# First tiles of a four-layer attention and MLP kernel: VectorE order, load order, one tile's transpose and the weight loads

## The chip, the cores and the metric

The kernel runs on one core of a Trainium2 chip. The metric is device time of one execution in microseconds (us). Before the change the median of 3 runs is 758.88 us (758.61 to 761.05).

The engines are TensorE (PE, matrix products; PEld is its weight load), VectorE (DVE), ScalarE (ACT), GpSimd (POOL) and SyncE (SP), which issues the DMAs here. Each engine takes its instructions in order, so an instruction that waits holds up all that stand behind it on its engine.

## The reference

`x` has 2048 rows of 576 values in bf16. Four layers follow one another, attention (A), MLP (B), A, B, all with the same weights, each on a layer norm of its input and with a residual sum:

```
def _A_ref(x, wqkv, wo):
    q, k, v = ...            # x @ wqkv, 32 heads of 18
    phi = lambda t: jnp.where(t > 0, t + 1, jnp.exp(t)) + 1e-6
    pq, pk = phi(q), phi(k)
    kv = jnp.einsum("bhsd,bhse->bhde", pk, v)
    z = jnp.einsum("bhsd->bhd", pk)
    num = jnp.einsum("bhqd,bhde->bhqe", pq, kv)
    den = jnp.einsum("bhqd,bhd->bhq", pq, z)[..., None] + 1e-6
    o = num / den
    return o... @ wo

def _B_ref(x, w1, b1, w2, b2):
    h = _gelu(jnp.einsum("bsd,df->bsf", _layernorm(x), w1) + b1)
    return jnp.einsum("bsf,fd->bsd", h, w2) + b2

x = x + _A_ref(_layernorm(x), A_wqkv, A_wo)
x = x + _B_ref(_layernorm(x), B_w1, B_b1, B_w2, B_b2)
...                          # the same two once more
```

## The kernel before

The rows are cut into 16 tiles of 128 (NT). Products over the 576 features need the normalised rows turned, features on the partitions: `yT` holds them in 5 blocks of 128 (KD). Layer 1 (li = 0) reads its rows from the input; each tile goes through a small pipeline, `LNPipe`, whose `tick` moves every tile in it one step on: statistics (DVE: two bn_stats and one bn_aggr, L391, L392, L398; or ACT: two passes that sum, L371 and L381), the reciprocal deviation (ACT with Ln and Exp for tiles 0 to 2, L422 and L424; else POOL with a power, L427), the normalisation (DVE for tiles 0 to 3, L440; POOL for the others, L436), and the turning. A tile below `XB` is turned by five PE transposes into PSUM (L494), which ACT copies to `yT` (L500); the others by one DMA transpose on SP (L483). `feed0` (L1162) puts a tile of layer 1 in and chooses its path.

Per tile layer 1 then makes the keys in two halves (`k_half`, five products each, L657), the feature map of the keys (an exponential on ACT, L544, and one maximum and minimum on DVE, L546), and, one tile later, the sums of rows by keys (`rows_by_keys`, L699: four chunks of 128 features and a tail, `k2_tail`). Between them stands one of the 20 query products (`q_proj`, five products, L625), with an exponential (L558) and an identity pass (L559) on ACT, both read from PSUM, and a minimum and a maximum on DVE (L564, L566). The query, key and transpose results share the four PSUM buffers of pool `ps_h`; the tail of the sums holds one of them to the end of the keys. A product whose turn comes needs a buffer that its last reader has left.

For the first tiles the order is written out by hand: instructions are entered under names (`s2a`, `s2b`, `g2`, `u2` for the statistics of tile 2, `n2` for its normalisation, `cd0` and `ca0` for the copies of tile 0's transposes, `e10` and `ma10` for the exponential and the maximum of tile 1's first key half), and `in_order` (L181) makes each follow the one before it. PE has its own written order (`pe`). `chained` (L160) does the same for the DMA issues of the beginning.

SP issues the loads: row tiles and the key, query and value weights first; then the DMA transposes in turn with `late_pieces` (L264), one of which `pre_a1_layer0` (L1177) takes off per tile from tile 4 on: nine pieces of w1 of 512 KB, the output weight `piece_wo`, two w1 tails, the first three pieces of w2, b1; b2 goes at the last tile. `last_pieces`, the last three of w2, went one by one at the last four tiles of layer 1's output stage (L1016). An issue also waits until the DMA eight issues before it has landed, since the DMAs take turns on eight semaphores.

After the keys come the sums of the second half, the denominators, the products of keys and values with the output weight (`kv_wo_half`, L769), the output products (L968) and the residual sums. The MLP then works on chunks of 512 rows: 9 groups of first products (`m1_group`, L1082) and second products over 36 blocks of the hidden values (L1144).

## Time and profile before

| | |
|---|---|
| median of 3 runs | 758.88 us |
| the profiled execution | 759.16 us |
| its span | 757.2 us |
| PE busy in the span | 750.6 us |
| DVE, ACT, POOL busy | 261.3, 323.3, 114.9 us |
| granted TensorE clock | 1.00 in the stages of layer 1 |
| DMA moved | 75.20 MB |

The span is that of the traced instructions; the profiled execution's own time is 1.92 us longer. In a row of the timeline stand the start, the duration of a run of equal instructions, engine, line, operation, what is written and read, and the count; in brackets the idle time of the engine just before and what ended it. A run of PE's reaches past the start of the next one, because products overlap. SPq rows are issues of DMAs, not the transfers. In the rows by stage each engine has its busy time and count, and at the end stand the granted clock, the mean busy share of the DMA engines and GB/s.

### The profile page before, as it was taken

Reading aid. Unit: us, or ns where it says so; the run is one execution under the profiler, and the core shown is the slowest. Engines: PE = TensorE matmul, PEld = TensorE weight load, DVE = VectorE, ACT = ScalarE, POOL = GpSimd, SP = SyncE. Lnnn points to the kernel's source line nnn. Section 1 sums busy time; section 2 is a strip of 40 time slices with the busy share of each in tenths; the row PEclk is TensorE's granted clock in tenths of the full one; section 3 lists DMA queues with packets and bytes.
Section 4 is the critical chain, followed back from the end, with each engine's and each line's share of the span. In section 5 each row is a group of like instructions: output and inputs, shape, how many; then the busy total and the mean of one; then the engine's idle time right before and its main releaser. Section 6 shows DMA issues by size and latency. Waiting matters only on the chain.

```text
span 757.2 us, 15677 instructions
## 1 busy us (share of the span) xinstructions
PE 750.6 (99%) x6555; PEld 484.7 (64%) x6555; DVE 261.3 (35%) x641; ACT 323.3 (43%) x722; POOL 114.9 (15%) x219
## 2 busy tenths in 40 slices
PE   8999999999999999999999999999999999999998
PEld 5677754774476457646777777457646754774476
DVE  7766824136034403401366567600230132000000
ACT  5767656105601640373057666660174036205600
POOL 4830313003010201200110004300020020001000
PEclk9999999999999999999999999999999999999999
DMA  8796692226313611411404147430240033011000
GB/s 241 172 246 159 200 350 65 71 65 182 82 40 94 166 51 48 121 54 32 127 24 118 32 137 256 173 83 16 87 106 17 16 126 83 9 32 56 1 9 24
DMA packets 83984, 75.20 MB, mean 99 GB/s; under 512 B 39882, under 2 KB 68554, under 8 KB 83914
## 3 DMA queue, kind: packets, MB, share of 16 engines
q1 hardware_dynamic: 83914, 74.21, 34.5%
q8 instruction: 51, 0.84, 0.5%
q14 instruction: 19, 0.16, 0.1%
HBM read 48.10 MB, written 24.77 MB: 96 GB/s over the span
## 4 chain that ended last, share of the span: by engine, by line
PE 95%; DMA 1%; ACT 1%; DVE 1%; POOL 1%; SPq 0%; issue 0%; POOLq 0%; DVEq 0%
PE m_ps L1144 36%; PE h_ps L1082 21%; PE hp_ps L1082 16%; PE q_ps L625 5%; PE k_ps L657 5%; PE k_ps L699 4%; PE wo_ps L968 3%; PE m_half L1144 1%; DMA xo<-x_d 1%; DMA x<-in_A_x_dram 1%; PE k_tail L699 0%; PE kv_ps L751 0%; ACT turned L846 0%; PE rden_ps L842 0%; PE den_ps L801 0%
## 5 line engine op out<-in xcount | busy, mean ns | idle before, releaser
L1144 PE MATMUL m_ps<-w_sb,hT 128*128 128x288 bf16 x2232 | 274.8, 286 | 0.0
L1144 PEld LDWEIGHTS <-hT 128*128 128x128 bf16 x2304 | 224.2, 98 | 60.4 <-issue 3.4
L1082 PEld LDWEIGHTS <-w_sb 64*128 64x128 bf16 x2304 | 124.5, 94 | 136.4 <-issue 1.9
L1082 PE MATMUL hp_ps<-yT,w_sb 64*128 64x512 bf16 x1152 | 178.0, 376 | 0.0
L1082 PE MATMUL h_ps<-yT,w_sb 64*128 64x512 bf16 x1152 | 148.0, 376 | 0.0
L1087 ACT COPY relay_sb<-relay_sb 128x1 f32<-128x1 f32 x144 | 28.5, 198 | 261.2 <-PE h_ps L1082 218.1
L1078 ACT ACTIVATE hT<-h_ps,b1T 128x512 bf16<-128x512 f32 x144 | 91.1, 683 | 43.8 <-PE h_ps L1082 43.8
L427 POOL TENSOR_TENSOR ln_rstd<-ln_u,neg_half 128x1 f32<-128x1 f32 x61 | 34.3, 563 | 412.3 <-DVE ln_u L409 209.4
L1078 ACT ACTIVATE hT<-hp_ps,b1T 128x512 bf16<-128x512 f32 x144 | 91.1, 692 | 0.0
L609 DVE TENSOR_TENSOR xbf<-m_ps,xo 128x576 bf16<-128x576 f32 x15 | 11.4, 757 | 212.9 <-PE m_ps L1144 212.9
L609 DVE TENSOR_TENSOR xo<-m_ps,xo 128x576 f32<-128x576 f32 x16 | 12.1, 757 | 168.2 <-PE m_ps L1144 168.2
L592 POOL TENSOR_TENSOR xo<-xo,b_bc 128x576 f32<-128x576 f32 x32 | 40.9, 1281 | 115.2 <-DMA xo<-x_d 85.3
L1082 PE MATMUL h_ps<-yT,w_tail 64*128 64x512 bf16 x144 | 54.1, 376 | 0.0
L1082 PE MATMUL hp_ps<-yT,w_tail 64*128 64x512 bf16 x144 | 54.1, 376 | 0.0
L625 PE MATMUL q_ps<-yT,wqkv_sb 128*126 128x512 bf16 (+1 forms) x200 | 49.4, 379 | 0.4 <-DVE pk L546 0.4
L657 PE MATMUL k_ps<-wqkv_sb,yT 128*128 128x288 bf16 x320 | 44.6, 286 | 0.3 <-DMA wqkv_sb<-in_A_wqkv_dram 0.2
L968 PE MATMUL wo_ps<-kvwo,pq 126*128 126x288 bf16 (+1 forms) x320 | 43.5, 286 | 0.6 <-DVE xo L609 0.4
L1082 PEld LDWEIGHTS <-w_tail 64*128 64x128 bf16 x288 | 27.1, 94 | 17.1
L657 PEld LDWEIGHTS <-yT 128*128 128x128 bf16 x320 | 31.0, 98 | 10.6 <-ACT yT L497 0.6
L968 PEld LDWEIGHTS <-pq 126*128 126x128 bf16 (+1 forms) x320 | 30.3, 97 | 9.6 <-issue 1.3
L558 ACT ACTIVATE phi_e<-q_ps 126x512 bf16<-126x512 f32 (+1 forms) x40 | 23.9, 596 | 23.6 <-PE q_ps L625 21.6
L625 PEld LDWEIGHTS <-wqkv_sb 128*126 128x126 bf16 (+1 forms) x200 | 25.7, 131 | 12.3 <-issue 1.0
(151 smaller groups left out, 562.5 us busy)
## 6 DMA issues: line engine op xcount, KB each, us to landing
xo<-x_d SPq DMA_DIRECT2D x48, 288.0 KB
x_d<-xo SPq DMA_DIRECT2D x32, 288.0 KB
xl<-x_d SPq DMA_DIRECT2D x24, 288.0 KB
y_d<-turned SPq DMA_DIRECT2D x40, 144.0 KB
w_sb<-in_B_w_dram SPq DMA_DIRECT2D x6, 864.0 KB
yT<-y_d SPq DMA_DIRECT2D x10, 512.0 KB
w_sb<-in_B_w_dram SPq DMA_DIRECT2D x9, 512.0 KB
x_d<-xn SPq DMA_DIRECT2D x16, 288.0 KB
```

Source lines behind the costliest of these rows:

```text
L427: nc.gpsimd.tensor_tensor(out=rstd[:], in0=it["u"][:], in1=neg_half[:], op=ALU.pow)
L558: exp = nc.scalar.activation(out=e_out, in_=ps_ap, func=ACT.Exp)
L592: nc.gpsimd.tensor_tensor(out=xo[:], in0=xo[:], in1=b2_bc[:], op=ALU.add)
L609: total = nc.vector.tensor_tensor(out=xn[:, cols].rearrange("p (h n) -> p h n", h=2), in0=halves, in1=xo[:, cols].rearrange("p (h n) -> p ...
L625: pe(nc.tensor.matmul(qp[0:GR[g], :], lhsT=wqkv_sb[:, k, GO[g]:GO[g] + GR[g]], rhs=yT[:, k, c * CA:(c + 1) * CA], start=(k == 0), stop=(k ...
L657: pe(nc.tensor.matmul(kp[:, 0:HALF], lhsT=yT[:, k, t * P:(t + 1) * P], rhs=wqkv_sb[:, k, D + half * HALF: D + (half + 1) * HALF], start=(k ...
L699: pe(nc.tensor.matmul(dst, lhsT=lhsT, rhs=pk, start=(t == 0), stop=(t == NT - 1)))
L968: pe(nc.tensor.matmul(wp[:, half, 0:HALF], lhsT=pq[(g, c)][0:GR[g], j * P:(j + 1) * P], rhs=kvwo[g][0:GR[g], half * HALF:(half + 1) * HALF ...
L1078: act_last["gelu"] = nc.scalar.activation(out=to, in_=ps, func=ACT.Gelu_apprx_tanh, bias=b1T[:, f:f + 1], scale=1.0).ins.name
L1082: mm = pe(nc.tensor.matmul(dst[n], lhsT=wt, rhs=mv, start=(seen[n] == 0), stop=(seen[n] == 8)))
L1087: relay = nc.scalar.copy(out=relay_sb[:, 1:2], in_=relay_sb[:, 0:1])
L1144: pe(nc.tensor.matmul(acc[half][:, 0:cols.stop - cols.start], lhsT=hT[f][:, j * P:(j + 1) * P], rhs=w2_sb[:, f, cols], start=(f == 0), sto ...
```

## The change

Six edits, all in layer 1 or in the loads that go with it:

- Row tile 2 is loaded ahead of the first half of the key weights instead of behind it.
- The written DVE order of the first tiles is another one; the normalisation of tile 2 now stands ahead of tile 3's statistics. PE makes tile 4's transposes between the first two query groups instead of behind both. The minimum and maximum of the second query group come later (`late=True`), and the four tail sums of tiles 0 to 3 go behind tile 5's transposes. Tile 4's keys join the written order.
- `XB` is 7: tile 7 is turned by DMA instead of PE.
- Statistics on ACT go to tiles 8, 11 and 14 instead of 9, 12 and 15.
- `piece_wo` goes behind all w1 pieces and both tails; two pieces are issued at tile 4 and none at tile 5, so the DMA transposes of tiles 7 and 8 stand next to each other.
- The last three w2 pieces are called up in the first groups of the MLP. On SP the first of them stands behind the same store as before, the other two one store later.

On each engine the built order changes in these places alone; PE has five matrix instructions and their five weight loads fewer. On ACT tile 8's two statistics passes now stand on both sides of the exponential of the third query group, ahead of its identity pass; before, tile 9's stood behind that group.

```
-        XB = 8
+        XB = 7
...
         load_x0(0)
         load_x0(1)
+        load_x0(2)
         load_wqkv(1, 0)
-        load_x0(2)
         load_wqkv(1, 1)
...
-        late_pieces = [(lambda i=i: piece_w1(i)) for i in range(4)] + [piece_wo] + \
-                      [(lambda i=i: piece_w1(i)) for i in range(4, 9)] + \
-                      [(lambda i=i: piece_w1_tail(i)) for i in range(2)] + [(lambda i=i: piece_w2(i)) for i in range(3)] + [piece_b1_dma]
+        late_pieces = [(lambda i=i: piece_w1(i)) for i in range(9)] + \
+                      [(lambda i=i: piece_w1_tail(i)) for i in range(2)] + [piece_wo] + [(lambda i=i: piece_w2(i)) for i in range(3)] + [piece_b1_dma]
...
+            def larger(dve_after=dve_after):
+                nc.vector.tensor_scalar(out=e[0:rows, 0:n], in0=e[0:rows, 0:n], scalar1=1.0, scalar2=1e-6,
+                                        op0=ALU.min, op1=ALU.add)
+                top = nc.vector.tensor_tensor(out=out_ap, in0=a[0:rows, 0:n], in1=e[0:rows, 0:n], op=ALU.max)
...
+            if late:
+                return larger
+            larger()
...
-                phi = q_proj(*q_left.pop(0), defer=True)
                 feed_and_tick(5, 1)
                 feed_and_tick(6, 2)
-                phi(after=first_ones["ca4"].ins.name)
-                in_order("s0a s0b g0 s1a s1b n0 g1 cd0 n1 s2a s2b g2 cd1 s3a ma00 n2 s3b g3 u3 ma10 s4a "
-                         "n3 ma11 ma20 s4b ma21 g4 u4 ma01 s5a s5b g5 u5 ma30 ma31")
+                phi = q_proj(*q_left.pop(0), defer=True)
+                lnp.tick(transposes=0)
+                first_max = phi(after=first_ones["ca4"].ins.name, late=True)
+                in_order("s0a s0b g0 s1a s1b n0 g1 s2a cd0 n1 s2b g2 cd1 ma00 n2 s3a s3b g3 u3 ma10 ma01 n3 ma11 ma20 "
+                         "s4a s4b g4 u4 ma21 ma31 s5a ma30 s5b g5 u5")
...
-                for t in range(4):
-                    rows_by_keys(t, 0, (4,))
                 for t in range(4, NT):
-                    keys(t)
+                    if t == 4:
+                        k_half(t, 0)
+                        first_max(dve_after=dve_last["phi"])
+                        k_half(t, 1)
+                        in_order("u5 s6a s6b g6 u6 ma40 ma41")
+                    else:
+                        keys(t)
                     pre_a1(t)
                     if t == 4:
-                        lnp.tick()
+                        lnp.tick(transposes=0)
                     masks(2)
                     if t > 4:
                         rows_by_keys(t - 1, 0)
+                    else:
+                        for one in range(4):
+                            rows_by_keys(one, 0, (4,))
...
-                if last_pieces and t >= NT - TPC:
-                    last_pieces.pop(0)()
...
                         self.m1_group(c, g)
+                        if last_pieces:
+                            last_pieces.pop(0)()
...
-                     stats="act" if t >= XB and t % 3 == 0 else "dve")
+                     stats="act" if t > XB and t % 3 == 2 else "dve")
...
-            if late_pieces:
+            for _ in range(2 if t == 4 else 0 if t == 5 else 1):
                 late_pieces.pop(0)()
```

## The prediction

> **What bounds the kernel now.** I read the page's first part, then the busy time of each engine by stage, then the instructions of TensorE (PE) in order of time, with what ended each idle stretch.
>
> ```profile
> span 757.2 us, 15677 instructions
> PE 750.6 (99%) x6555; PEld 484.7 (64%) x6555; DVE 261.3 (35%) x641; ACT 323.3 (43%) x722; POOL 114.9 (15%) x219
> ```
> ```profile
> core 0: us, PE busy (x) PEld busy (x) DVE busy (x) ACT busy (x) POOL busy (x), PEclk, DMA share, GB/s
> 5.34:26.47 21.13, 19.63 (x159) 14.25 (x159) 16.45 (x53) 15.19 (x37) 10.19 (x27) 1.00 0.76 224
> 26.47:57.00 30.53, 30.53 (x207) 21.87 (x205) 20.39 (x64) 20.98 (x51) 15.14 (x44) 1.00 1.05 232
> ```
>
> PE is busy for 99% of the span, and from 26.47 to 57 us for all of it. What this change can win without leaving out matrix work lies before 26.47 us, where PE is idle for 21.13 - 19.63 = 1.50 us. Every edit that touches another engine or a queue after that point can only lose, or move something that already waits for nobody.
>
> ```profile
> start us, us, engine line op out<-in xcount [idle before <-releaser]
> 7.59 1.40 PE L657 MATMUL k_ps<-wqkv_sb,yT 128*128 128x288 bf16 x10 [0.16 <-DMA wqkv_sb<-in_A_wqkv_dram]
> 9.61 0.45 PE L494 MATMUL tp<-ident,x 128*128 128x128 bf16 x5 [0.62 <-DVE x L440]
> ...
> 17.65 0.66 PE L699 MATMUL k_tail<-pk,x 128*65 128x289 bf16 x4
> 18.14 1.39 PE L657 MATMUL k_ps<-wqkv_sb,yT 128*128 128x288 bf16 x10
> 19.36 0.44 PE L494 MATMUL tp<-ident,x 128*128 128x128 bf16 x5
> 20.20 1.24 PE L625 MATMUL q_ps<-yT,wqkv_sb 128*126 128x512 bf16 x5 [0.39 <-DVE pk L546]
> 21.27 1.39 PE L657 MATMUL k_ps<-wqkv_sb,yT 128*128 128x288 bf16 x10
> 22.61 0.44 PE L494 MATMUL tp<-ident,x 128*128 128x128 bf16 x5
> ...
> 24.58 1.39 PE L657 MATMUL k_ps<-wqkv_sb,yT 128*128 128x288 bf16 x10
> 26.19 0.44 PE L494 MATMUL tp<-ident,x 128*128 128x128 bf16 x5 [0.22 <-ACT phi_a L559]
> 26.47 0.29 PE L699 MATMUL k_tail<-pk,x 128*65 128x289 bf16 x1
> 27.08 1.24 PE L625 MATMUL q_ps<-yT,wqkv_sb 128*72 128x512 bf16 x5
> 28.16 1.39 PE L657 MATMUL k_ps<-wqkv_sb,yT 128*128 128x288 bf16 x10
> ```
>
> The groups are, from the code: keys of a tile (L657, ten products), its transposes (L494, five), queries (L625, five), sums by keys (L699). Transposes at 9.61, 19.36, 22.61 and 26.19 belong to tiles 2, 5, 6, 7; keys at 18.14, 21.27, 24.58, 28.16 to tiles 4, 5, 6, 7. A group's duration reaches past the start of the next, so I measure by starts: five transposes take 26.47 - 26.19 = 0.28 us, and a tile's keys 1.22 us, from tile 11:
>
> ```profile
> 39.97 1.39 PE L657 MATMUL k_ps<-wqkv_sb,yT 128*128 128x288 bf16 x10
> 41.19 0.29 PE L699 MATMUL k_tail<-pk,x 128*65 128x289 bf16 x1
> ```
>
> By starts the losses are: tile 2's transposes 9.61 - (7.59 + 1.22) = 0.80; the queries 20.20 - (19.36 + 0.28) = 0.56; tile 6's transposes 22.61 - (21.27 + 1.22) = 0.12; tile 7's 26.19 - (24.58 + 1.22) = 0.39. With the 0.28 us of tile 7's own transposes, 2.15 us are within reach of this change.
>
> **The change part by part.** (a) VectorE (DVE) order and load order.
>
> ```profile
> 8.19 0.20 ACT L424 ACTIVATE ln_rstd<-ln_rstd 128x1 f32<-128x1 f32 x1
> 8.39 0.46 DVE L391 BATCH_NORM_STATS2 ln_st<-x 128x6 f32<-128x288 bf16 x1 [0.64 <-DMA x<-in_A_x_dram]
> 8.77 0.44 DVE L546 SCALAR_TENSOR_TENSOR pk<-k_ps,y_ring 128x288 bf16<-128x288 f32 x1
> 9.13 0.42 DVE L440 TENSOR_SCALAR x<-x,ln_mv,ln_rstd 128x576 bf16<-128x576 bf16 x1
> ```
>
> DVE stands 0.64 us in front of tile 3's first statistics until that tile lands; behind it in the queue stand the first key maximum and the normalisation of tile 2, for which PE waits. In the changed order both stand ahead of tile 3. Tile 2's scale is there at 8.19 + 0.20 = 8.39, so its normalisation runs at about 8.42 and ends 0.42 later, at 8.84; its transposes start 0.06 after that, as now (9.13 + 0.42 = 9.55 to 9.61), at 8.90. Gain 9.61 - 8.90 = 0.71. Its cover: tile 2 must land in time, and it is now loaded ahead of the first key weights; these move back by one issue, and the first key product of all may wait for them. I price that at nothing, since tile 2 and these weights together end where they ended before; bounds 0 and +0.6 us, the latter the issue that they move back:
>
> ```profile
> 2.79 0.58 SPq L190 DMA_DIRECT2D x<-in_A_x_dram  x1
> ```
>
> (b) The stall at 20.20 waits for DVE's maximum on tile 4's first half, which frees a PSUM buffer. The change puts that maximum ahead of the maximum of the second query group, leaves tile 4 further ahead of it, and moves the four tail products (18.14 - 17.65 = 0.49 us) behind tile 5's transposes, where they cover the rest. I take the whole 0.56 us as won, less 0.09 us that I expect before tile 4's keys: its transposes now start one query group earlier, but their eviction on ScalarE (ACT) still stands behind the first query group's two passes. Bounds 0 and 0.56.
>
> (c) Which tiles take their statistics on ACT. Tile 9 had them there, now tile 8.
>
> ```profile
> 21.97 0.59 ACT L559 ACTIVATE phi_a<-q_ps 126x512 bf16<-126x512 f32 x1
> 22.73 0.69 ACT L371 ACTIVATE ln_dump<-x 128x576 bf16<-128x576 bf16 x1
> 24.26 0.81 ACT L381 ACTIVATE ln_dump<-x,ln_mv 128x576 bf16<-128x576 bf16 x1
> 25.03 0.62 ACT L558 ACTIVATE phi_e<-q_ps 126x512 bf16<-126x512 f32 x1
> 25.51 0.63 ACT L559 ACTIVATE phi_a<-q_ps 126x512 bf16<-126x512 f32 x1
> ```
>
> This is the same trap one tile earlier. The squares (L381) delay the query passes by 25.03 - 24.26 = 0.77 us; the identity pass ends at 25.51 + 0.63 = 26.14, it frees the buffer that the next transposes take, and these start at 26.19: that is the 0.39 us before tile 7. In the changed order tile 8's first pass falls into ACT's idle time before the query group at 20.20, but its squares stand between that group's exponential and its identity pass, and tile 6's transposes take that group's buffer. Today that identity pass ends (21.97 + 0.59 = 22.56) when tile 6's turn comes; 0.77 us later it makes PE wait. Loss 0.77; bounds 0 (if ACT runs far enough ahead) and 0.77 + 0.69 = 1.46, with the first pass not hidden either.
>
> (d) Tile 7 turned by DMA. PE loses five transposes and the wait before them: gain 0.28 + 0.39 = 0.67. The price is a landing time.
>
> ```profile
> 23.28 0.82 POOL L436 TENSOR_SCALAR x<-x,ln_rstd,ln_nmr 128x576 bf16<-128x576 bf16 x1
> 25.09 0.82 POOL L436 TENSOR_SCALAR x<-x,ln_rstd,ln_nmr 128x576 bf16<-128x576 bf16 x1
> 25.94 1.33 SPq L483 DMA_TRANSPOSE yT<-x  x1
> 34.67 1.39 SPq L483 DMA_TRANSPOSE yT<-x  x1
> ```
> ```profile
> 24.00:25.94 1.94, 1.94 (x14) 1.28 (x13) 0.56 (x2) 1.94 (x5) 1.73 (x5) 1.00 0.00 0
> 28.20:28.60 0.40, 0.40 (x5) 0.33 (x4) 0.29 (x2) 0.24 (x1) 0.40 (x1) 1.00 0.17 13
> ```
>
> GpSimd (POOL) normalises tile 7 at 23.28 and tile 8 at 25.09. Tile 8's transpose is issued at 25.94 into idle DMA engines (share 0.00) and has moved its bytes by 28.60: 2.66 us. The transposes behind weight pieces have longer: tile 11's, issued at 34.67, is at the latest there at 39.97, when that tile's keys start without a wait, 5.30 us. Tile 7's goes first of all, into the same idle stretch: I take 2.66. Its normalisation ends between 22.9 (1.2 us earlier, with the gains of a and b) and 24.10 (as now), so it lands between 25.6 and 26.8; its keys start at 28.16 - 1.08 = 27.08. Covered, by 0.3 us at the least. With 5.30 us it lands between 28.2 and 29.4, and PE loses 1.1 to 2.3 us. On SyncE's queue tile 8's transpose stands behind it; that waits for its normalisation longer than for the 1.33 us of issue.
>
> The Trainium skill (VectorE: DVE Perf Modes, "Rules for kernel authors") advises TensorE for a 128x128 transpose where PSUM will do and the crossbar DMA otherwise, and "The three transpose paths" gives 390 ns against 1309 ns. That speaks against (d): five blocks one after the other would be 6.5 us, an estimate from that page; tile 7 would land up to 24.10 + 6.5 = 30.6, and its keys start 2.4 us later than now instead of 1.08 earlier. The trace shows 0.28 us on PE and 2.66 us by DMA for five blocks, so it doesn't agree, and I don't follow the page.
>
> (e) Output weight behind the transposes, the weight pieces placed anew. No bytes are added. Its first reader, and the state of the DMA engines ahead of it:
>
> ```profile
> 71.58 0.29 PE L769 MATMUL kvwo_half<-wo_sb,kvT 126*126 126x288 bf16 x1
> 68.00:79.00 11.00, 11.00 (x101) 8.40 (x101) 7.41 (x21) 8.22 (x18) 0.21 (x1) 1.00 0.18 53
> ```
>
> The output weight still goes ahead of b2, three w2 pieces and b1, and even those have drained when the share falls to 0.18. Zero, with more than 3 us of cover. Between tile 10's and tile 11's transposes a 512 KB piece replaces the 648 KB of the output weight, which helps tile 11. The last w2 pieces go to SyncE a few stores later, near 100 us; the second MLP product begins here, and reads them last:
>
> ```profile
> 135.21 6.05 PE L1144 MATMUL m_ps<-w_sb,hT 128*128 128x288 bf16 x48
> ```
>
> Zero too, with tens of microseconds of cover. The sum: 0.71 + 0.56 - 0.09 - 0.77 + 0.67 = 1.08 us. The profiled execution, 759.16 us (757.24 of span and 1.92 around it), becomes 758.1. The median of the runs is 0.28 lower, 758.88; on it I forecast **757.8**.
>
> **The rivals.** *The ACT trap doesn't close* (c costs nothing, nor the 0.09): gain 1.94, 756.9. For it: ACT is busy 15.19 of 21.13 us there, so it has room. Against: its order is fixed, and the squares can't pass the exponential.
>
> *The gain is given back at the turned tiles 8 to 15.* DMA share is 1.05 from 26.47 on; if the weight traffic and not PE's progress sets when tiles land, PE catches up with the queue and waits, at tile 11 first. Gain 0, 758.9. Against: each transpose is issued when POOL ends a normalisation (25.09 + 0.82 = 25.91 to 25.94), and these follow the keys, which come earlier.
>
> *Slower: tile 7 lands late.* One mechanism: its transpose takes the 5.30 us of tile 11's, from the normalisation's present end of 24.10: 29.40, and the keys of tile 7 start there instead of at 28.16. From then on all is 1.24 us later: 760.1. It is slower than before as soon as tile 7 lands after 28.16. For it: a two-microsecond DMA path replaces 0.28 us of PE. Against: the DMA engines are idle when it is issued.
>
> **How the numbers follow.** Forecast 0.60; ACT trap open 0.16; given back 0.12; slower 0.12. The range goes from the second case to the last: 756.8 to 760.2. About 0.3% (2.3 us) is what a measurement of this kernel can tell from no change, so faster means below 756.6 and slower above 761.2. The 2.15 us within reach stay under that bound, and only noise on the second case carries it over: faster 0.08. Slower needs the late landing and a second stall with it: 0.09. Same 0.83.
>
> **What would show it.** Tile 2's transposes at 8.9 us; the third query group near 19.0 with no wait on DVE; tile 6's transposes near 22.2 after a wait of 0.8 to 0.9 on ACT's identity pass; no transposes of tile 7 on PE and its keys near 27.1 without a wait on DMA; no idle PE until 57; the first MLP product 1.1 us earlier than now. A wait on DMA at the first key product, at tile 7's or a later tile's keys, or at the first reader of the output weight would make the prediction wrong, and each would show its size there.

## The result and the profile after

The changed kernel takes 758.08 us (median of 20 runs, 757.86 to 758.96); the kernel before took 758.88 us in as many runs of the same comparison (758.61 to 761.05). The ratio is 0.9986, with a 95% interval of 0.998 to 0.9992: 0.80 us less. The interval leaves out 1, so the kernel is faster, but by less than the 0.3% below which the prediction counts a change as none. The forecast was 757.8 us.

The profiled execution took 758.96 us, the longest of the 20. First its first part, then TensorE's instructions in order of time (start, duration of the run of equal instructions, engine, line, operation, tiles, count; in brackets the idle time before it and what ended it). In the changed kernel L493 are the transposes, L660 the keys, L628 the queries, L702 the sums by keys.

```profile
span 757.1 us, 15669 instructions
PE 750.8 (99%) x6550; PEld 484.4 (64%) x6550; DVE 261.3 (35%) x641; ACT 323.3 (43%) x721; POOL 114.6 (15%) x219
```
```profile
5.74 1.06 PE L221 MATMUL warm_ps<-y_ring 128*128 128x512 bf16 x2
6.59 1.09 PE L660 MATMUL k_ps<-wqkv_sb,yT 128*128 128x288 bf16 x5
...
9.45 0.45 PE L493 MATMUL tp<-ident,x 128*128 128x128 bf16 x5
...
19.57 1.24 PE L628 MATMUL q_ps<-yT,wqkv_sb 128*126 128x512 bf16 x5
...
22.74 0.44 PE L493 MATMUL tp<-ident,x 128*128 128x128 bf16 x5 [0.70 <-ACT phi_a L558]
...
30.72 1.39 PE L660 MATMUL k_ps<-wqkv_sb,yT 128*128 128x288 bf16 x10
```

Tile 2's transposes start at 9.45 instead of 9.61, the third query group (19.57) no longer waits for VectorE, tile 6's transposes wait for ScalarE's identity pass as forecast, and tile 7 has no transposes on TensorE. But most of the gain is missing at tile 2 already. TensorE is late there because it ran slowly: the last two warm-up products took 1.06 us and tile 0's first five key products 1.09 us. A second profile of the same kernel (e1 below) shows the same stretch without that:

```profile
5.78 0.69 PE L221 MATMUL warm_ps<-y_ring 128*128 128x512 bf16 x2
6.34 0.79 PE L660 MATMUL k_ps<-wqkv_sb,yT 128*128 128x288 bf16 x5
...
8.89 0.45 PE L493 MATMUL tp<-ident,x 128*128 128x128 bf16 x5
...
19.02 1.24 PE L628 MATMUL q_ps<-yT,wqkv_sb 128*126 128x512 bf16 x5
20.10 1.39 PE L660 MATMUL k_ps<-wqkv_sb,yT 128*128 128x288 bf16 x10
22.18 0.44 PE L493 MATMUL tp<-ident,x 128*128 128x128 bf16 x5 [0.70 <-ACT phi_a L558]
...
22.58 0.66 PE L702 MATMUL k_ps<-pk,x 128*128 128x289 bf16 x4
23.24 1.24 PE L628 MATMUL q_ps<-yT,wqkv_sb 128*126 128x512 bf16 x5
...
27.24 1.39 PE L660 MATMUL k_ps<-wqkv_sb,yT 128*128 128x288 bf16 x10
...
30.16 1.39 PE L660 MATMUL k_ps<-wqkv_sb,yT 128*128 128x288 bf16 x10
```

The kernel before has these three rows for the fourth query group, tile 8's keys and the first MLP product; that product starts at 99.09 in the second profile of the changed kernel, shown after it.

```profile
23.50 1.24 PE L625 MATMUL q_ps<-yT,wqkv_sb 128*126 128x512 bf16 x5
...
31.20 1.39 PE L657 MATMUL k_ps<-wqkv_sb,yT 128*128 128x288 bf16 x10
...
100.14 1.04 PE L1082 MATMUL h_ps<-yT,w_sb 64*128 64x512 bf16 x8
```
```profile
99.09 1.04 PE L1091 MATMUL h_ps<-yT,w_sb 64*128 64x512 bf16 x8
```

So the gain is 1.04 us at tile 8's keys and 1.05 us at the first MLP product, against 1.08 forecast. The first profile has 31.20 - 30.72 = 0.48 us at tile 8's keys and nothing left at the first MLP product (100.16 against 100.14). Single profiles also differ by what happens later, where the change has no part. In the first profile after, two waits of TensorE stand that the second one lacks:

```profile
90.53 0.65 PE L979 MATMUL wo_ps<-kvwo,pq 126*128 126x288 bf16 x4 [0.29 <-DVE xn L612]
```
```profile
465.61 0.23 PE L493 MATMUL tp<-ident,y_ring 128*128 128x128 bf16 x1 [0.41 <-POOL y_ring L466]
```

Two times must therefore be kept apart below. The one is the median of the runs, always less the median of the kernel before in the same comparison. The other is read in the trace: the start of the third query group, which holds all that happened before it, a slow start too, and the stretch from there to tile 8's keys, which doesn't depend on the start. The kernel before needs 31.20 - 20.20 = 11.00 us for that stretch, the changed kernel 30.72 - 19.57 = 11.15 in the first profile and 30.16 - 19.02 = 11.14 in the second.

| kernel | median, us | less before | ratio, 95% interval | third query group | from there to tile 8's keys |
|---|---|---|---|---|---|
| before | 758.88 | | | 20.20 | 11.00 |
| changed | 758.08 | -0.80 | 0.9986 (0.998 to 0.9992) | 19.57 | 11.15 |
| e1 changed again | 757.94 | -0.90 | 0.999 (0.9981 to 0.9999) | 19.02 | 11.14 |
| e2 ScalarE statistics as before | 758.53 | -0.31 | 0.9998 (0.9989 to 1.0007) | 19.05 | 11.64 |
| e3 tile 7 on TensorE | 758.26 | -0.58 | 0.9994 (0.9984 to 1.0003) | 18.98 | 11.53 |
| e4 order and load alone | 758.39 | -0.45 | 0.9996 (0.9987 to 1.0005) | 19.20 | 11.42 |
| e7 tile 2's load late | 758.22 | -0.44 | 0.9993 (0.9985 to 1.0002) | 19.29 | 11.14 |
| e8 tile 3 first | 758.12 | -0.54 | 0.9992 (0.9984 to 1.0) | 19.46 | 11.14 |
| e14 weights as before | 757.85 | -0.81 | 0.9986 (0.9978 to 0.9994) | 19.00 | 11.14 |
| e12 squares later | 757.51 | -0.98 | 0.9986 (0.9977 to 0.9995) | 18.99 | 10.88 |
| e11 memset on VectorE | 757.69 | -0.80 | 0.9988 (0.9979 to 0.9997) | 18.97 | 11.15 |
| e10 both | 757.51 | -0.98 | 0.9984 (0.9975 to 0.9993) | 19.48 | 10.88 |
| e9 statistics as before, memset | 757.67 | -0.82 | 0.9983 (0.9975 to 0.9992) | 19.65 | 10.86 |
| e13 no statistics of tile 8 on ScalarE | 757.06 | -1.60 | 0.998 (0.9972 to 0.9989) | 19.03 | 10.60 |

The kernel before had 758.84 in the comparison of e1 to e4, 758.49 in that of e9 to e12 and 758.66 in that of e7, e8, e13 and e14. The intervals are up to 0.0019 wide, some 1.4 us, and nearly all of them overlap: a difference of two variants rests on the medians and on the rows of the trace together, not on the intervals.

### The profile page after: what moved, and what is told of

The parts are those of the page before. It is cut to its first block, busy times and chain, and to the rows that moved or that the text cites. A ratio compares the mean times of both kernels' runs of the same rounds, so it can differ in the third digit from the quotient of the medians.

```text
span 757.1 us, 15669 instructions
## 1 busy us (share of the span) xinstructions
PE 750.8 (99%) x6550; PEld 484.4 (64%) x6550; DVE 261.3 (35%) x641; ACT 323.3 (43%) x721; POOL 114.6 (15%) x219
## 4 chain that ended last, share of the span: by engine, by line
PE 96%; ACT 1%; POOL 1%; DMA 1%; DVE 1%; issue 0%; POOLq 0%; DVEq 0%
PE m_ps L1155 36%; PE h_ps L1091 21%; PE hp_ps L1091 16%; PE q_ps L628 6%; PE k_ps L660 5%; PE k_ps L702 4%; PE wo_ps L979 3%; PE m_half L1155 1%; PE warm_ps L221 1%; DMA x_d<-xn 1%; PE k_tail L702 1%; PE tp L493 0%; PE kv_ps L754 0%; ACT turned L849 0%; PE den_ps L804 0%
## 5 line engine op out<-in xcount | busy, mean ns | idle before, releaser
L628 PE MATMUL q_ps<-yT,wqkv_sb 128*126 128x512 bf16 (+1 forms) x200 | 49.5, 379 | 0.1
L660 PE MATMUL k_ps<-wqkv_sb,yT 128*128 128x288 bf16 x320 | 45.1, 287 | 0.0
L660 PEld LDWEIGHTS <-yT 128*128 128x128 bf16 x320 | 31.1, 98 | 10.7 <-ACT yT L496 0.7
L628 PEld LDWEIGHTS <-wqkv_sb 128*126 128x126 bf16 (+1 forms) x200 | 25.7, 131 | 11.9 <-issue 0.7
```

The source lines that it names most:

```text
L628: pe(nc.tensor.matmul(qp[0:GR[g], :], lhsT=wqkv_sb[:, k, GO[g]:GO[g] + GR[g]], rhs=yT[:, k, c * CA:(c + 1) * CA], start=(k == 0), stop=(k ...
L660: pe(nc.tensor.matmul(kp[:, 0:HALF], lhsT=yT[:, k, t * P:(t + 1) * P], rhs=wqkv_sb[:, k, D + half * HALF: D + (half + 1) * HALF], start=(k ...
```

## The experiments

Theory A, in the first four runs, is the prediction's own account: the parts are worth what its rows say, and what the first profile after lacks doesn't belong to the change. The rivals stand with each run. Diffs are against the changed kernel.

**e1, the changed kernel once more**, without an edit.

> The changed kernel once more, as the measure for the other three and for a second profile. Theory A (the waits of the first 27 us decide, and what the first profile shows behind them is of that execution alone): 0.8 us below the kernel before, tile 6's transposes again wait 0.7 to 0.9 us for ACT's identity pass, the wait of the output products for a VectorE sum near 90 us (0.46 us by starts) is absent or elsewhere, and the slow start (first key products at 0.19 us each instead of 0.12) is absent too. Theory B (both belong to the change): both come back at the same places with the same sizes.

The steps of the prediction came out in the rows shown above: 8.89, 19.02, 22.18, no wait of tile 7's keys on DMA, and none of the two later waits. Theory A holds in that they don't belong to the change. They aren't of that one execution alone either: the wait near 465 us comes back, with the same 0.41 us, in the profiles of e3, e4, e9, e10, e12 and e13, and a slow start in those of e9 and e10. The second profile took 757.65 us, 0.29 below its median, as the first was 0.88 above its own.

**e2, statistics on ScalarE for tiles 9, 12 and 15 again.**

```
-                     stats="act" if t > XB and t % 3 == 2 else "dve")
+                     stats="act" if t > XB and t % 3 == 0 else "dve")
```

> The changed kernel with ACT's statistics on tiles 9, 12 and 15 again. Theory A: the squares no longer stand ahead of the third query group's identity pass, tile 6's transposes lose their wait of 0.86 us, and the time is 0.7 to 0.9 us below that of the changed kernel. Rival: the transposes of tile 6 wait for POOL's normalisation or another buffer as soon as the identity pass is early, or the wait goes to the next query group; then the time is within 0.2 us of the changed kernel.

It is 0.59 us slower than the changed kernel of the same comparison (0.90 - 0.31) instead of faster. TensorE's and then GpSimd's rows of this kernel:

```profile
21.47 0.44 PE L493 MATMUL tp<-ident,x 128*128 128x128 bf16 x5
...
28.99 0.28 PE L702 MATMUL k_tail<-pk,x 128*65 128x289 bf16 x1 [0.64 <-POOL pk L666]
```
```profile
27.27 0.82 POOL L435 TENSOR_SCALAR x<-x,ln_rstd,ln_nmr 128x576 bf16<-128x576 bf16 x1
28.05 0.85 POOL L87 TENSOR_SCALAR_AFFINE_SELECT narrow<-narrow 128x35 bf16<-128x35 bf16 x2
28.84 0.10 POOL L666 MEMSET pk<- 128x1 bf16 x1
```

Tile 6's transposes no longer wait, but the sums of that tile wait later for a memset of one column (0.10 us), which sets the ones beside the keys. It stands on GpSimd behind a whole normalisation and two mask steps. The rival, that the wait goes elsewhere, was right in kind and too small in size.

**e3, tile 7 on TensorE.**

```
-        XB = 7
+        XB = 8
...
-                     stats="act" if t > XB and t % 3 == 2 else "dve")
+                     stats="act" if t >= XB and t % 3 == 2 else "dve")
```

> The changed kernel with tile 7 turned by PE again, ACT's statistics kept on tiles 8, 11 and 14. Theory A: PE gets five transposes back (0.28 us), and since the squares no longer stand ahead of these, no wait with them: 0.3 us above the changed kernel. Rival (the wait of 0.39 us that stood before tile 7's transposes comes back with them): 0.6 to 0.7 us above it. Rival (tile 7's DMA transpose is itself late and holds PE): the same or faster than the changed kernel.

The median is 0.32 us above the changed kernel's, as expected, and the stretch 0.39 us longer. Tile 7's transposes are back, and there is no wait in brackets before them:

```profile
24.29 1.39 PE L660 MATMUL k_ps<-wqkv_sb,yT 128*128 128x288 bf16 x10
25.62 0.44 PE L493 MATMUL tp<-ident,x 128*128 128x128 bf16 x5
```

By starts 25.62 - (24.29 + 1.22) = 0.11 us are lost there, where the kernel before lost 0.39.

**e4, the kernel before with the new order and tile 2's load alone.** Against the changed kernel it undoes the other four parts:

```
-        XB = 7
+        XB = 8
...
-        late_pieces = [(lambda i=i: piece_w1(i)) for i in range(9)] + \
+        late_pieces = [(lambda i=i: piece_w1(i)) for i in range(4)] + [piece_wo] + \
...
-                     stats="act" if t > XB and t % 3 == 2 else "dve")
+                     stats="act" if t >= XB and t % 3 == 0 else "dve")
...
-            for _ in range(2 if t == 4 else 0 if t == 5 else 1):
+            if late_pieces:
```

> The kernel before with the new order of the first tiles and the new load of tile 2 alone; tile 7 on PE, statistics on tiles 9, 12 and 15, output weight and w2 pieces at their old places. Theory A: it wins the two stalls (0.71 and 0.56 us, less 0.1), but the wait before tile 7's transposes stays: 1.0 to 1.2 us below the kernel before, so faster than the changed kernel by 0.2 to 0.4. Rival (the order alone wins little because the first tiles wait for their loads): 0.2 to 0.6 us below the kernel before.

It brings 0.45 us, the rival's size but not for the rival's reason. At the third query group it is 1.00 us ahead of the kernel before, and of that it gives back 0.42 by tile 8's keys: new small waits stand behind, the largest of them before the fourth query group. Theory A's wait before tile 7's transposes doesn't stay: 25.28 - (23.95 + 1.22) = 0.11 us are lost there instead of 0.39, although tile 9 still has its squares on ScalarE. They now end before the fourth query group's products do (the last row is ScalarE's; that group's exponential follows at 24.15).

```profile
22.87 1.24 PE L629 MATMUL q_ps<-yT,wqkv_sb 128*126 128x512 bf16 x5 [0.20 <-DVE pk L546]
...
25.28 0.44 PE L494 MATMUL tp<-ident,x 128*128 128x128 bf16 x5
```
```profile
23.27 0.81 ACT L381 ACTIVATE ln_dump<-x,ln_mv 128x576 bf16<-128x576 bf16 x1
```

**e12, tile 8's squares behind the third query group's identity pass.** The two passes of tile 8's statistics on ScalarE stay; only the second one goes behind the identity pass that frees the PSUM buffer.

```
...
+                    if t == 4:
+                        tc.add_manual_dep(first_ones["sq8"].ins, act_last["phi"], NOSYNC, reason="identity pass first")
```

> The changed kernel, with only tile 8's squares on ScalarE ordered behind the third query group's identity pass; the memset of pk stays on GpSimd. Theory (two constraints): the wait of tile 6's transposes goes (start 21.4), and 0.5 to 0.7 us of it comes back a few us later as a wait of the tail sums on pk's memset (GpSimd) or of tile 8's keys on their DMA transpose; tile 8's keys at 29.8 to 30.1; 0 to 0.4 us below the changed kernel. Rival (the memset was in the way only because tile 9 took its statistics on ScalarE): no wait on GpSimd, tile 8's keys at 29.3, 0.8 us below the changed kernel.

The wait is gone (tile 6's transposes at 21.41), and the stretch falls by 0.26 us, not by 0.86. What comes back doesn't wait for GpSimd's memset, as the theory had it, but for VectorE; and the rival's 0.8 us fail too.

```profile
21.41 0.44 PE L493 MATMUL tp<-ident,x 128*128 128x128 bf16 x5
...
22.95 1.24 PE L628 MATMUL q_ps<-yT,wqkv_sb 128*126 128x512 bf16 x5 [0.49 <-DVE pk L545]
...
39.51 1.40 PE L660 MATMUL k_ps<-wqkv_sb,yT 128*128 128x288 bf16 x10 [0.71 <-DMA yT<-x]
```

Why, ScalarE's order shows, first in the changed kernel (second profile), then in this one:

```profile
20.79 0.77 ACT L380 ACTIVATE ln_dump<-x,ln_mv 128x576 bf16<-128x576 bf16 x1
...
21.55 0.59 ACT L558 ACTIVATE phi_a<-q_ps 126x512 bf16<-126x512 f32 x1
22.02 0.71 ACT L543 ACTIVATE phi_e<-k_ps 128x288 bf16<-128x288 f32 x2
```
```profile
20.76 0.59 ACT L558 ACTIVATE phi_a<-q_ps 126x512 bf16<-126x512 f32 x1
21.24 0.78 ACT L380 ACTIVATE ln_dump<-x,ln_mv 128x576 bf16<-128x576 bf16 x1
...
22.00 0.71 ACT L543 ACTIVATE phi_e<-k_ps 128x288 bf16<-128x288 f32 x2
```

The key exponentials (L543) start at 22.02 there and at 22.00 here. ScalarE does the same work in this stretch in either order, VectorE's key maxima follow these exponentials, and the fourth query group waits for a maximum to free its buffer. Only the place of the wait has moved.

The same profile shows the other rival of the prediction once: tile 11's keys wait 0.71 us for their DMA transpose. Among the profiles it is the only one, and that execution took 758.65 us, the longest of its 11.

**e11, the memset of the ones column on VectorE** from tile 5 on, alone.

```
+                        if t < 5:
+                            pool_last["pk"] = nc.gpsimd.memset(pk[:, HALF:HALF + 1], 1.0).ins.name
+                        else:
+                            nc.vector.memset(pk[:, HALF:HALF + 1], 1.0)
```

> The changed kernel with only the one-column memset of pk on VectorE from tile 5 on. Theory: in the changed kernel nobody waits for that memset, since the wait of tile 6's transposes on ScalarE stands ahead of it, so nothing changes: within 0.2 us of the changed kernel, tile 6's transposes at 22.18 after 0.70 on ScalarE, tile 8's keys at 30.1 to 30.2. Rival (VectorE is short of time in this stretch, and one more instruction of 0.1 to 0.2 us in each tile delays its maxima): 0.2 to 0.5 us slower, with waits on VectorE's pk.

No difference, as the theory expected: 0.80 below the kernel before, and the stretch at 11.15. In the changed kernel nobody waits for that memset.

**e10, both edits, e12's and e11's.**

> The changed kernel, with two edits: tile 8's squares on ScalarE are ordered behind the third query group's identity pass, and the one-column memset of pk goes from GpSimd to VectorE from tile 5 on. Theory (two constraints stand one behind the other: the squares ahead of the identity pass cost 0.86 us, and once they are gone the memset queued on GpSimd behind a normalisation costs 0.6 us; only with both removed does the time fall): tile 6's transposes at about 21.4, no TensorE wait on ScalarE or GpSimd before 27 us, tile 8's keys at 29.2 to 29.4 against 30.16 in the changed kernel, 0.7 to 1.0 us below the changed kernel of the same call (some 757.1). Rival (tile 8's squares, now later, delay its normalisation, so its DMA transpose lands after its keys' turn): tile 8's keys wait on a DMA and start at 30.0 or later; 757.8 to 758.2.

Both expectations miss: 0.18 us below the changed kernel of that comparison (e11 stands for it, at -0.80), and the same stretch of 10.88 us as with the squares alone, with the same wait of 0.49 us on VectorE and none on DMA. The memset is not the second constraint of the changed kernel; ScalarE's total is.

**e9, e2 with the memset on VectorE.**

> The changed kernel with the ScalarE statistics on tiles 9, 12, 15 again, as in the run with that alone, and the one-column memset of pk on VectorE from tile 5 on. Theory: the wait of 0.64 us of tile 6's tail sums on GpSimd's memset, which gave that run its loss, is gone; tile 8's keys at 29.6 to 30.1 instead of 30.69; 757.3 to 757.8, so 0.6 to 1.0 us below the run with the statistics alone and at or below the changed kernel. Rival (the memset is only the last of several things that come late there, the two waits of about 0.2 us on VectorE and tile 7's landing stand behind it): 758.2 to 758.5, no gain.

The wait for the memset is gone and with it 0.51 us of time (from -0.31 to -0.82) and 0.78 us of the stretch (11.64 to 10.86). This shows the memset to be what made e2 slow. By the median it only draws level with the changed kernel, although its stretch is 0.28 us shorter. e9 and e11 differ in the tiles with statistics on ScalarE alone: -0.82 and -0.80 by the medians, 10.86 and 11.15 in the stretch.

**e13, no statistics of tile 8 on ScalarE** (tiles 11 and 14 keep theirs there), with e11's memset.

```
-                     stats="act" if t > XB and t % 3 == 2 else "dve")
+                     stats="act" if t > XB + 1 and t % 3 == 2 else "dve")
...
```

> The changed kernel with the memset of pk on VectorE from tile 5 on, and with tile 8's statistics on VectorE, so that ScalarE takes them only for tiles 11 and 14. Putting the squares later removed the wait of 0.86 us but brought only 0.3 us, since ScalarE then handed the exponentials of tile 6's keys over as late as before. Theory (ScalarE's total of work between 19 and 23 us is the limit there; the two passes of tile 8, some 1.3 us, must leave that stretch): no TensorE wait between 19 and 27 us, third and fourth query groups at about 19.0 and 22.5, tile 8's keys at 29.3 to 29.5 when TensorE's start is as in the changed kernel's second profile, 0.6 to 0.8 us less than the changed kernel of these calls, unless tile 11's DMA transpose gives it back. Rival (VectorE has no room either: it has 0.6 us of idle time there and takes on 0.9 us): a wait of 0.3 to 0.6 us on VectorE's pk or on tile 7's or tile 8's DMA transpose, 0 to 0.3 us less than the changed kernel.

The best of all: 757.06 us, 1.60 below the kernel before, 0.8 below the changed one, and 0.55 us less in the stretch than e11, from which it differs in this line alone. Where the rest of the 0.8 comes from isn't shown. A wait on VectorE is left, the rival's kind, and shorter than it expected:

```profile
22.71 1.24 PE L628 MATMUL q_ps<-yT,wqkv_sb 128*126 128x512 bf16 x5 [0.21 <-DVE pk L545]
```

VectorE takes tile 8's statistics in where it had stood idle (the first row is VectorE's in the changed kernel's second profile, 0.95 us of idle time ahead of the query group's maximum), and ScalarE, rid of both passes, hands over the key exponentials 0.74 us earlier (the second row is ScalarE's in e13, 21.28 instead of 22.02):

```profile
22.17 0.65 DVE L567 TENSOR_TENSOR pq<-phi_a,phi_e 126x512 bf16<-126x512 bf16 x1 [0.95 <-ACT phi_a L558]
```
```profile
21.28 0.72 ACT L543 ACTIVATE phi_e<-k_ps 128x288 bf16<-128x288 f32 x2
```

**e7, tile 2's load behind the first key weights again.**

```
         load_x0(1)
-        load_x0(2)
         load_wqkv(1, 0)
+        load_x0(2)
```

> The changed kernel, with tile 2's load issued behind the first key weights again, as in the kernel before; all else as changed. Theory (the load move belongs to part (a): VectorE now handles tile 2's statistics ahead of the first normalisation's eviction and stands there until tile 2 lands, one issue of about 0.6 us later): the first key products or tile 2's transposes 0.3 to 0.6 us later than 6.3 and 8.9, and 0.3 to 0.6 us slower than the changed kernel. Rival (both pieces land together, and the place of the load is of no account): within 0.15 us of the changed kernel, tile 2's transposes at 8.8 to 9.0.

It costs 0.36 us against the changed kernel's -0.80, at the low end of the theory. VectorE, whose order has tile 2's statistics early, stands 0.94 us before they can start, and tile 2's transposes are 9.17 - 8.89 = 0.28 us later; the stretch behind is unchanged. This profile also has a slow start (tile 0's keys at 6.59 instead of 6.34), but the wait for tile 2 is enough by itself: tile 1's normalisation stands behind those statistics, ends at 6.84 + 0.42 = 7.26, and tile 1's transposes follow at 7.32, when TensorE could have begun them at 6.59 + 0.62 = 7.21 (0.62 is what tile 0's keys take by starts in the second profile). The first two rows are VectorE's, the third is TensorE's:

```profile
6.28 0.46 DVE L390 BATCH_NORM_STATS2 ln_st<-x 128x6 f32<-128x288 bf16 x1 [0.94 <-DMA x<-in_A_x_dram]
...
6.84 0.42 DVE L439 TENSOR_SCALAR x<-x,ln_mv,ln_rstd 128x576 bf16<-128x576 bf16 x1
```
```profile
9.17 0.45 PE L493 MATMUL tp<-ident,x 128*128 128x128 bf16 x5
```

**e8, tile 3's first statistics ahead of tile 2's normalisation again.**

```
-                in_order("s0a s0b g0 s1a s1b n0 g1 s2a cd0 n1 s2b g2 cd1 ma00 n2 s3a s3b g3 u3 ma10 ma01 n3 ma11 ma20 "
+                in_order("s0a s0b g0 s1a s1b n0 g1 s2a cd0 n1 s2b g2 cd1 s3a ma00 n2 s3b g3 u3 ma10 ma01 n3 ma11 ma20 "
```

> The changed kernel, with the first half of tile 3's statistics ahead of the first key maximum and of tile 2's normalisation in VectorE's order, as in the kernel before. Theory (part (a): VectorE stands before tile 3 until it lands, and tile 2's normalisation behind it comes 0.7 us later): tile 2's transposes at 9.5 to 9.6, 0.6 to 0.7 us slower than the changed kernel. Rival (the next wait takes it over: with 0.7 us less of progress, TensorE no longer waits for ScalarE at 21.5): tile 2's transposes late as above, but the wait of tile 6's transposes 0.3 to 0.7 us shorter and only 0 to 0.3 us slower.

It costs 0.26 us by the median. In the trace tile 2's transposes are 9.33 - 8.89 = 0.44 us later, less than the theory's 0.6 to 0.7. Tile 3 landed earlier in this execution: VectorE begins its statistics at 8.12 (the first row), in the kernel before at 8.39, and these 0.27 us are the size of the shortfall. The rival's range holds the time, but its mechanism fails: the wait of tile 6's transposes is as long as ever (0.70), and the stretch is 11.14.

```profile
8.12 0.46 DVE L390 BATCH_NORM_STATS2 ln_st<-x 128x6 f32<-128x288 bf16 x1 [0.45 <-DMA x<-in_A_x_dram]
```
```profile
9.33 0.45 PE L493 MATMUL tp<-ident,x 128*128 128x128 bf16 x5 [0.26 <-DVE x L439]
...
22.62 0.44 PE L493 MATMUL tp<-ident,x 128*128 128x128 bf16 x5 [0.70 <-ACT phi_a L558]
```

**e14, the weight traffic of the kernel before**: the output weight among the w1 pieces, the last w2 pieces at the stores of the last tiles.

```
-        late_pieces = [(lambda i=i: piece_w1(i)) for i in range(9)] + \
-                      [(lambda i=i: piece_w1_tail(i)) for i in range(2)] + [piece_wo] + [(lambda i=i: piece_w2(i)) for i in range(3)] + [piece_b1_dma]
+        late_pieces = [(lambda i=i: piece_w1(i)) for i in range(4)] + [piece_wo] + \
+                      [(lambda i=i: piece_w1(i)) for i in range(4, 9)] + \
+                      [(lambda i=i: piece_w1_tail(i)) for i in range(2)] + [(lambda i=i: piece_w2(i)) for i in range(3)] + [piece_b1_dma]
...
+                if last_pieces and t >= NT - TPC:
+                    last_pieces.pop(0)()
...
-                        if last_pieces:
-                            last_pieces.pop(0)()
```

> The changed kernel, with the weight traffic of the kernel before: the output weight between the fourth and the fifth piece of w1, and the last w2 pieces at the stores of the last group of tiles. Theory (part (e) is worth nothing): within 0.2 us of the changed kernel, no new wait on DMA, the first MLP product at the same time. Rival (the output weight's 648 KB between two transposes delay tile 11, which has only about half a microsecond of cover): a wait of 0.3 to 1.0 us of tile 11's keys on their DMA transpose at about 38 us, and as much slower.

No difference, as the theory expected: 0.81 us below the kernel before, the first MLP product at 99.12 instead of 99.09, and no wait of TensorE on a transpose by DMA. The two pieces at tile 4 and none at tile 5 stay as changed; no run undoes these alone.

## Why the prediction was right, and where it was not

The time was forecast at 757.8 and measured at 758.08; the account below goes by the second profile, whose start resembles that of before. The steps (a) and (b) came out at their places. (c) and (d) came out as rows of the trace, but not as the worth of the edits, and that the sum fits so well is in part luck.

(a) 0.71 us at tile 2's transposes: 9.61 to 8.89 is 0.72. The normalisation of tile 2 runs as forecast (8.42 to 8.84):

```profile
8.40 0.43 DVE L439 TENSOR_SCALAR x<-x,ln_mv,ln_rstd 128x576 bf16<-128x576 bf16 x1 [0.30 <-ACT ln_rstd L423]
```

The size was right and its split wrong. The prediction gave all of it to VectorE's order and priced the load at nothing. Its fear for the first key product didn't come true (6.34, before 6.36). But with the new order and the old load (e7) the transposes start at 9.17, 0.44 before 9.61; the load brings the other 0.28. In the new order VectorE stands in front of tile 2 itself, so tile 2 must also come earlier. No run has the old order with the new load; e8 undoes one step of the order.

(b) 0.56 - 0.09 = 0.47 us: the third query group starts 20.20 - 19.02 = 1.18 earlier, which is 0.46 beyond (a). The wait is gone, as forecast; that the 0.09 fits is luck, since no wait stands before tile 4's keys and the difference is lost in small steps between groups. No run separates the order of the maxima from the place of the tail sums.

(c) 0.77 us of loss: mis-sized. The wait was as described, 22.18 - (20.10 + 1.22) = 0.86, where the kernel before lost 0.12, and behind it the fourth query group lost 23.24 - (22.58 + 0.49) = 0.17 more, since the key exponentials and maxima had been held up too. In these rows 0.74 + 0.17 = 0.91 us are lost. But that isn't what the edit costs. With the statistics back on tile 9 (e2) the kernel gets 0.59 us slower, since the memset then holds TensorE; with the memset out of the way tile 9 is the better choice by only 0.02 us in the medians and 0.29 in the stretch (e9 against e11). And the step "these squares delay the identity pass by 0.77" took a busy engine for a wrong order: e12 undoes just that delay and gets 0.26 back in the stretch, e13 takes both passes off ScalarE and gets 0.55. What set the end was the sum of ScalarE's work between the query group and the key exponentials.

(d) 0.28 + 0.39 = 0.67 us: between the fourth query group and tile 7's keys the kernel gained (28.16 - 27.24) - (23.50 - 23.24) = 0.66. The size was right, the cause of most of the 0.39 wrong: with tile 7 back on TensorE only 0.11 us is lost before its transposes, with the squares on tile 8 (e3) and on tile 9 (e4) alike. So 0.28 of that wait was gone with the new order and load already, and the transpose by DMA itself is worth 0.39 in the trace (0.32 in the medians). Its landing was covered. SyncE's row for the two transposes of tiles 7 and 8 in the second profile, and the row of one stage, in which the DMA engines rest (share 0.00):

```profile
22.57 3.46 SPq L482 DMA_TRANSPOSE yT<-x  x2
```
```profile
25.00:26.00 1.00, 1.00 (x10) 0.81 (x9) 0.66 (x3) 1.00 (x4) 1.00 (x4) 1.00 0.00 0
```

Ahead of that stage, from 23.80 on, they had worked; so tile 7's bytes were moved by 25.00, 2.43 us after the issue, near the 2.66 that the prediction took. Tile 7's keys started at 27.24 without a wait, 4.67 us after the issue, so the transpose took no longer than that; in e13 the same keys start 26.71 - 23.36 = 3.35 us after the issue, also without a wait. This excludes the 6.5 us that were worked out, as an estimate, from the Trainium skill (VectorE: DVE Perf Modes, "The three transpose paths"); the trace doesn't agree with one block after the other.

(e) Nothing: right (e14).

Taken together, two errors cancel. Order and load alone (e4), which (a) and (b) price at 1.18 us, bring 0.45 by the medians and 31.20 - 30.62 = 0.58 at tile 8's keys (30.62 is 19.20 + 11.42): the third query group comes early as forecast (19.20, of which 0.18 against 19.02 is a slower start), but 0.42 is given back behind it. The other parts, priced at -0.77 + 0.67 = -0.10, bring the rest, 0.90 - 0.45 = 0.45 by the medians and 11.42 - 11.14 = 0.28 in the stretch. The prediction added up waits as if each removed one were won for good.

Of the 1.04 us in the trace at tile 8's keys the medians show 0.80 to 0.90. The rest stays open. The spread behind tile 8's keys is large enough for it: from there to the end of the span the first profile after takes 757.1 - 30.72 = 726.4 us, the second 755.7 - 30.16 = 725.5, the kernel before 757.2 - 31.20 = 726.0.

Of the rivals, the trap that doesn't close (756.9) did not come, and e12 shows that placing the squares later alone doesn't open it; e13, which takes them away, reaches 757.06. The gain wasn't given back at tiles 8 to 15 (1.04 us at tile 8's keys, 1.05 at the first MLP product), and late landing of tile 7 did not occur. The loss at tile 11 was seen once, in e12, where the kernel ran further ahead than the changed one: the cover there is thin.

## What to carry to other kernels

A wait behind a wrongly placed instruction is worth at most what is left when that instruction stands anywhere else on the same engine: add up the engine's work up to its next handover before pricing a reorder, and move the work to an idle engine if the sum is the limit. A wait that a trace shows is not the worth of the edit that removes it: undo the edit alone, and see where the next wait stands. An order that makes an engine look at a tile earlier needs that tile's load earlier as well; the two belong to one edit. Look for tiny instructions on a busy queue (here a memset of 0.10 us) that a matrix product needs.

## What the hardware showed that was not expected

The moment at which TensorE reaches full rate differs between executions of the same program. Tile 0's first five key products took 1.09 us in the first profile after and 0.79 us in the second, the two warm-up products before them 1.06 and 0.69; the granted clock of the stage is 1.00 in both:

```profile
5.34:26.47 21.13, 20.32 (x155) 14.36 (x155) 16.62 (x52) 15.10 (x37) 10.81 (x29) 1.00 0.80 230
```
```profile
5.34:26.47 21.13, 20.18 (x159) 14.67 (x160) 17.20 (x54) 15.39 (x37) 11.15 (x31) 1.00 0.81 234
```

It is worth 0.55 us at the third query group (19.57 against 19.02), half of what the whole change brings; e9 and e10 show it as well (19.65 and 19.48). The Trainium skill (TensorE: Matmul & The Clock Gate, "Part 1: The HAM clock gate (the "warmup" mystery)") says that the array starts at half rate and is released at the end of a window of about 3.4 us that runs freely, so that the number of slow products differs from run to run. The rows agree with it; the column of the granted clock doesn't show it.

GpSimd's small copy ahead of a group of transposes took 0.84 us in the first profile after, where it made TensorE wait at 465.61, and 0.30 us in the second:

```profile
464.72 0.84 POOL L466 COPY y_ring<-y_ring 128x64 bf16<-128x64 bf16 x1
```
```profile
463.32 0.30 POOL L466 COPY y_ring<-y_ring 128x64 bf16<-128x64 bf16 x1
```

In the first, VectorE had begun two instructions of one line 0.01 us before the copy, and the copy ended 0.10 us after these:

```profile
464.71 0.75 DVE L855 TENSOR_TENSOR pq<-pq,turned 126x512 bf16<-126x512 bf16 x2
```

In the second, the copy had begun 0.13 us before VectorE's next instruction, which is one of another line. All 14 profiles divide in this way: in seven these two begin 0.01 us before the copy, and it takes 0.84 us; in the other seven, the kernel before among them, the copy is 0.13 us ahead of VectorE and takes 0.30. That the copy waits for VectorE is an inference from these rows; no run changes the order of the two.
